# Reordering the start of a fused delta-rule attention and two-layer MLP kernel, with the first MLP product cut into two halves of tokens

## The chip, the cores and the metric

The kernel runs on one core of a Trainium2 chip. The metric is the device time of one execution in microseconds (us). Engines are named as the profile names them: PE is TensorE (PEld its weight loads), DVE is VectorE, ACT is ScalarE, POOL is GpSimd, SP is SyncE, whose queue (SPq) issues nearly all the DMAs. A changed kernel counts here as different from the one before when the times differ by more than 0.3%.

## The reference

Inputs are q, k, v of shape (4, 8, 768, 48) and beta of shape (4, 8, 768), and the weights of two MLPs. For each batch and head a 48x48 state runs over the 768 tokens, and its output feeds the MLPs:

```
k_n = k / (norm(k) + 1e-6)
for t in range(S):
    y[t]  = q[t] @ state
    v_old = k_n[t] @ state
    state = state + beta[t] * outer(k_n[t], v[t] - v_old)
x = y as (3072, 384)
g = elu(x @ w_in);              x1  = g @ w_out        # 384 -> 2048 -> 384
h = x1 @ w2_in
g = h * sigmoid(1.702 * h);     out = g @ w2_out
```

## The kernel before, in words

**Attention.** The tokens of a sequence are cut into 12 chunks of 64 (`c`), and two chunks make a pass (`p`, 6 of them: 4 batches x 128 tokens = 512 columns). Inside a chunk the recurrence is solved in closed form: `gram` gives k.k products (PE, copied out by ACT in one whole copy and two part copies, `far`), `inverse` inverts the triangular matrices of a pass row by row with small DVE instructions (lists of steps: `start`, `take`, `diag`, `root`, `better`, `norm`, `scale`, the rows `step` or `step16`, `finish`, `turn`), `join16` (`left`, `right`), `m1` and `m2` put the blocks together on PE. Then per chunk: `kq` and `mask` (scores), `nv` (v scaled by the norm), `ks` (k times the state, subtracted from v on DVE at L567), `w` (copied out into the tiles su), `state` (the next state, added on DVE at L609), and `ya`, `yb` (the output; `y_out` splits it into xh on ACT and xl on DVE, L655 and L656).

**MLP.** A unit is one pass and one of 16 slices of 128 hidden columns. `up` makes 9 matmuls of 512 columns into a PSUM tile h (two buffers), `elu1` (two ACT instructions) and `elu2` (DVE, L761) follow, `high` (ACT cast to gh, L770) and `low` (DVE, gl, L773) split the result in two numbers, and two units later (`LAG = 2`) `down` makes 9 matmuls into acc0 to acc2. 192 units in all: 96 of layer 0, 96 of layer 1.

**Weights.** `prep` splits each weight slice likewise, once per slice: `rebase` (ACT), `shift` and `rest` (DVE, L714 and L717), `high` (ACT cast to wt, L724) and `low` (POOL, L728 in layer 0). In the list `conv` three entries belong to a slice: shift, rest with high, and low.

**What sets the order.** Everything is issued in an order written by hand; each engine works its own list in order. The code ahead of the units (L931 to L1005) is written out call by call; `also(n)` takes the next n steps of the second inverse. From then on each unit t has lists of things to issue: `fill` (after elu1), `mid` (before elu2), `end` (after down), `tail` (after high). A slot number s in the tables stands for the unit s//2, in `mid` if s is even and in `end` if it is odd. `spread` deals the steps of an inverse out over a stretch of units by the room that `taken` or `slack` leaves.

**PSUM tiles that are waited for.** `wide()` is one tile ps_w of two banks with a single buffer: `gram`, `kq`, `ks`, `w`, `state`, `m2` and y share it, so each waits until the one before has been copied out. While `early` holds, y of chunks 0 and 1 uses the two h buffers instead.

Of the kernel before, what the change touches and what calls it, by code (L numbers as in the profile page):

```python
# [19 lines left out]
P = 128  # L20
NP = S // P
# [10 lines left out]
class Kernel:  # L32
# [433 lines left out]
    def chunk(self, c):  # L466
# [218 lines left out]
    def prep(self, layer, ms, pools):  # L685
# [46 lines left out]
        for j, m in enumerate(ms):  # L732
            t = [lambda m=m: shift(m), lambda m=m: (rest(m), high(m))]
# [3 lines left out]
        steps.append(lambda: low(ms[-1]))  # L737
        return [lambda gate=False, m=m: load(m, gate) for m in ms], [lambda m=m: rebase(m) for m in ms], steps

    def up(self, wt, x, act_fn):  # L740

        nc = self.nc
        xh, xl = x
        hps = self.ps_m.tile([P, TB], F32, name="h", tag="h")
        i = 0
        for k in range(NK):
            for part, src in ((0, xh), (0, xl), (1, xh)):
                nc.tensor.matmul(  # L748
                    hps, wt[:, part, k * P:(k + 1) * P], src[:, k], start=(i == 0), stop=(i == 3 * NK - 1)
                )  # L750
                i += 1
# [105 lines left out]
    def schedule(self):  # L857
# [23 lines left out]
        def spread(where, u0, u1, fns, sizes=None):  # L881
# [3 lines left out]
            if u0 in slack:  # L885
                left = [max(0.2, slack.get(u, 0.0) + (2.8 if u > NM - 3 else 1.2)) for u in range(u0, u1)]
# [31 lines left out]
        loads, bases, conv = self.prep(0, range(NM), lambda m: (self.wp, "wt"))  # L918
        join = {c: self.later(lambda c=c: self.join16(c, home), 6) for c in range(6)}
# [66 lines left out]
        run(conv[0], conv[1], c0["ks"], c0["w"], c1["nv"], conv[2], bases[2], c0["state"])  # L986
# [3 lines left out]
        run(c0["ya"], c1["ks"], conv[3])  # L990
# [34 lines left out]
        for slot in (0, 2, 29, 32):  # L1025
# [3 lines left out]
        at(end, 7, lambda: self.load_v(3))  # L1029
# [5 lines left out]
        for p in range(2, NP):  # L1035
# [3 lines left out]
                (8, a, "kq"), (9, a, "t2"), (10, a, "m1"), (11, a, "ks"), (12, a, "m2"), (14, a, "w"),  # L1039
# [3 lines left out]
            late = 2 if p in self.FINE else 0  # L1043
# [78 lines left out]
    def passes(self, at, spread, half, fill, p, grams, steps, spare=None):  # L1122
# [116 lines left out]
```

## Time and profile before

| | |
|---|---|
| median of 3 runs | 991.79 us (989.93 to 992.45) |
| profiled execution, its own time | 990.37 us |
| its span, first to last instruction | 988.6 us (1.77 us of its time lie outside) |
| mean granted TensorE clock | 0.984 of full speed |
| busy: PE, DVE, ACT, POOL | 941.7, 594.4, 464.2, 83.1 us |
| instructions | 25639 |

Busy times are sums over the whole span. The MLP fills PE from about 92 us on, the attention of later passes runs between its units until about 500 us, and what lies ahead of 92 us is a chain through several engines. So a stretch has to be looked at by itself. The granted clock is 1.00 at 2.4 GHz and 0.50 at 1.2 GHz.

### The profile page before, as it was taken

How to read it: one execution, taken by the hardware profiler on the slowest of the kernel's cores; microseconds unless marked ns; L12 is line 12 of the kernel's file. 1: busy time of each engine (PE TensorE's matmuls, PEld its weight loads, DVE VectorE, ACT ScalarE, POOL GpSimd, SP SyncE). 2: the span in 40 equal slices, each digit the busy share in tenths (PEclk: the TensorE clock that was granted, in tenths of full speed). 3: DMA queues.
4: the chain of work that ended last, by engine and by line, in shares of the span. 5: the costliest groups of instructions: out<-in, count | busy, mean ns of one | idle time of the engine just before them, and what ended most of it. 6: DMA issues, size and time to landing. Idle time of an engine off the chain costs nothing.

```text
span 988.6 us, 25639 instructions
## 1 busy us (share of the span) xinstructions
PE 941.7 (95%) x11520; PEld 773.2 (78%) x11520; DVE 594.4 (60%) x1048; ACT 464.2 (47%) x753; POOL 83.1 (8%) x72
## 2 busy tenths in 40 slices
PE   4866899999999999999999999999999999999998
PEld 4755677778878887888887888888888888888886
DVE  6886887677987877886445676733333333333332
ACT  6636475644374465444446675533333233333332
POOL 3021252010010001000000100101001001010000
PEclk9977999999999999999999999999999999999999
DMA  7263342303211230210114801010010010100000
GB/s 240 88 208 104 108 154 91 114 4 92 83 56 58 74 98 19 92 44 34 34 49 157 371 1 64 1 54 11 1 65 1 1 64 1 64 1 1 33 1 32
DMA packets 20174, 68.33 MB, mean 69 GB/s; under 512 B 3168, under 2 KB 4704, under 8 KB 20064
## 3 DMA queue, kind: packets, MB, share of 16 engines
q1 hardware_dynamic: 19920, 66.56, 20.0%
q8 instruction: 90, 1.47, 0.6%
q14 instruction: 20, 0.16, 0.1%
q10 hardware_dynamic: 144, 0.13, 0.0%
HBM read 57.25 MB, written 9.44 MB: 67 GB/s over the span
## 4 chain that ended last, share of the span: by engine, by line
PE 85%; DVE 8%; ACT 4%; issue 2%; DMA 0%; POOL 0%; ACTq 0%; DVEq 0%; POOLq 0%
PE h L748 38%; PE acc L785 27%; PE accn L785 10%; PE ps_w L562 1%; PE ps_w L504 1%; PE ps_w L579 1%; PE ps_w L602 1%; PE ps_w L629 1%; PE ps_w L203 1%; DVE tmp L317 1%; PE ps_w L645 1%; ACT z L193 1%; DVE t L761 1%; DVE W L322 1%; DVE x L515 1%
## 5 line engine op out<-in xcount | busy, mean ns | idle before, releaser
L748 PE MATMUL h<-xh,wt 128*128 128x512 f32 x1152 | 396.4, 398 | 0.0
L785 PE MATMUL acc<-gh,wt 128*128 128x512 f32 x864 | 292.6, 393 | 0.5 <-DVE xo L846 0.5
L748 PEld LDWEIGHTS h<-xh,wt 128*128 128x128 f32 x1152 | 218.5, 190 | 48.1 <-DVE xl L656 0.2
L748 PE MATMUL h<-xl,wt 128*128 128x512 f32 x576 | 226.6, 393 | 0.0
L773 DVE TENSOR_TENSOR gl<-t,gh 128x512 fp32r<-128x512 f32 x192 | 138.7, 722 | 93.8 <-ACT gh L770 93.6
L785 PEld LDWEIGHTS acc<-gh,wt 128*128 128x128 f32 x864 | 162.7, 188 | 35.7 <-issue 0.9
L770 ACT CAST gh<-t 128x512 fp32r<-128x512 f32 x192 | 119.3, 621 | 118.8 <-DVE t L761 62.2
L785 PE MATMUL acc<-gl,wt 128*128 128x512 f32 x432 | 168.7, 390 | 0.0
L767 DVE TENSOR_TENSOR t<-t,h 128x512 f32<-128x512 f32 x96 | 66.0, 687 | 168.9 <-ACT t L764 168.9
L764 ACT ACTIVATE t<-h 128x512 f32<-128x512 f32 x96 | 57.3, 597 | 187.2 <-PE h L748 187.2
L748 PEld LDWEIGHTS h<-xl,wt 128*128 128x128 f32 x576 | 109.5, 190 | 21.1
L757 ACT ACTIVATE t<-h 128x512 f32<-128x512 f32 x96 | 57.4, 598 | 100.3 <-PE h L748 99.8
L785 PE MATMUL accn<-gh,wt 128*128 128x512 f32 x288 | 96.4, 389 | 0.0
L761 DVE SCALAR_TENSOR_TENSOR t<-t,h 128x512 f32<-128x512 f32 x96 | 65.6, 684 | 51.0 <-ACT t L758 50.5
L785 PEld LDWEIGHTS acc<-gl,wt 128*128 128x128 f32 x432 | 81.4, 188 | 16.1
L785 PEld LDWEIGHTS accn<-gh,wt 128*128 128x128 f32 x288 | 54.1, 188 | 11.3
L758 ACT ACTIVATE t<-t 128x512 f32<-128x512 f32 x96 | 60.7, 632 | 3.1
L812 POOL TENSOR_TENSOR xl<-x1r,xh 128x512 fp32r<-128x512 f32 x18 | 24.1, 1339 | 407.4 <-ACT xh L811 314.4
L785 PE MATMUL accn<-gl,wt 128*128 128x512 f32 x144 | 56.0, 389 | 0.0
L728 POOL TENSOR_TENSOR wt<-w,wt 128x768 fp32r<-128x768 f32 x16 | 31.5, 1974 | 70.7 <-ACT wt L724 70.7
L515 DVE TENSOR_TENSOR x<-ps_w,mask_p 64x512 f32<-64x512 f32 x44 | 30.2, 687 | 11.2 <-PE ps_w L504 10.7
L717 DVE SCALAR_TENSOR_TENSOR w<-raw,w 128x768 uint32<-128x768 uint32 x32 | 35.2, 1101 | 0.9
(190 smaller groups left out, 832.6 us busy)
## 6 DMA issues: line engine op xcount, KB each, us to landing
raw<-in_w SPq DMA_DIRECT2D x32, 768.0 KB, 7.6
kt<-in_kT SPq DMA_DIRECT2D x12, 512.0 KB, 4.5
x<-in_qT SPq DMA_DIRECT2D x24, 256.0 KB, 4.2
kg<-in_kT SPq DMA_DIRECT2D x9, 512.0 KB, 4.8
kn<-in_kn SPq DMA_DIRECT2D x12, 384.0 KB, 3.5
x1d<-xo SPq DMA_DIRECT2D x12, 384.0 KB, 2.9
x1r<-x1d SPq DMA_DIRECT2D x6, 768.0 KB, 4.7
vn<-in_vn SPq DMA_DIRECT2D x11, 384.0 KB, 3.4
```

What stands on the lines that cost most here:

```text
L515: v.tensor_tensor(out=g["x"][k][self.tok(k), 8 * hf:8 * hf + 8], in0=i, in1=self.mask_p[t].unsqueeze(1).to_broadcast(list(i.shape)), op=AL ...
L717: v.scalar_tensor_tensor(out=bits[m], in0=words(m, 0), scalar=29, in1=bits[m], op0=ALU.logical_shift_right, op1=ALU.bitwise_or)
L728: (v if layer else nc.gpsimd).tensor_tensor(out=wt[:, 1], in0=bits.pop(m).bitcast(F32), in1=wt[:, 0].bitcast(F32), op=ALU.subtract)
L748: nc.tensor.matmul(hps, wt[:, part, k * P:(k + 1) * P], src[:, k], start=(i == 0), stop=(i == 3 * NK - 1))
L757: nc.scalar.activation(out=t, in_=hps, func=AF.Relu, scale=-1.0)
L758: nc.scalar.activation(out=t, in_=t, func=AF.Exp, scale=-1.0)
L761: nc.vector.scalar_tensor_tensor(out=t, in0=t, scalar=-1.0, in1=hps, op0=ALU.add, op1=ALU.max)
L764: nc.scalar.activation(out=t, in_=hps, func=AF.Sigmoid, scale=1.702)
L767: nc.vector.tensor_tensor(out=t, in0=t, in1=hps, op=ALU.mult)
L770: nc.scalar.copy(gh, t)
L773: nc.vector.tensor_tensor(out=gl, in0=t, in1=gh.bitcast(F32), op=ALU.subtract)
L785: self.nc.tensor.matmul(self.acc[c], wt[:, part, DM + c * P:DM + (c + 1) * P], src, start=(m == 0 and i == 0), stop=(m == NM - 1 and i == 2),)
```

## The change

The change touches only the order of work, the places of a few PSUM tiles, and one product that is cut in two:

- **Start.** nv of chunk 1 goes ahead of the first weight conversion; the ACT cast `high` of a slice is taken out of `conv` into a list `highs` and stands later; `low` of slice 0 (POOL) goes ahead of y of chunk 0; norm and scale of the second inverse go ahead of `w` of chunk 1, and six row steps (12 DVE instructions) follow it instead of norm, scale and four.
- **Unit 0 in halves.** The new method `first` makes the 9 matmuls of `up` for a range of tokens. The first 256 tokens (chunk 0) are multiplied ahead of `ya` of chunk 1, the other 256 inside unit 0. y of chunk 1 goes to the tiles acc2 and ps_b, since h is now held by the halves.
- **Units 0 to 2.** `state` of chunk 1 goes from the middle of unit 2 to the middle of unit 0, and into acc0 and acc1 instead of ps_w. The two `gram` of pass 2 go from units 0 and 1 to units 1 and 2, each with both of its `far` copies at once. Weight `high` goes into `tail`, behind gh.
- **Later tables.** Items of chunks 2 and 3 move by up to three slots (nv 8 to 7, nv of chunk 3 18 to 21, ks 21 to 22, w 23 to 24, state 25 to 26, y 27 to 28); the `gram` of pass 3 go one slot later; m2 goes ahead of ks in passes 2, 4 and 5 (in pass 3 it already was); pass 5 goes one slot later up to w of its second chunk; `spread` carries a shortage of room over to the next unit.

The core of the diff:

```
-            if first:
+            if c < 2:
                 ps = self.banks(0)
...
-            if self.early:
+            if first:
                 st["y"] = [self.bank(True) for _ in range(2)]
+            elif self.early:
+                st["y"] = [self.ps_m.tile([P, TB], F32, name="acc2", tag="acc2", bufs=1), self.bank()]
...
-            t = [lambda m=m: shift(m), lambda m=m: (rest(m), high(m))]
+            t = [lambda m=m: shift(m), (lambda m=m: (rest(m), high(m))) if layer else (lambda m=m: rest(m))]
...
+    def first(self, wt, x, r, hps=None):
+        xh, xl = x
+        if hps is None:
+            hps = self.ps_m.tile([P, TB], F32, name="h", tag="h")
+        i = 0
+        for k in range(NK):
+            for part, src in ((0, xh), (0, xl), (1, xh)):
+                self.nc.tensor.matmul(
+                    hps[:, r], wt[:, part, k * P:(k + 1) * P], src[:, k, r], start=(i == 0), stop=(i == 3 * NK - 1)
+                )
...
-        run(conv[0], conv[1], c0["ks"], c0["w"], c1["nv"], conv[2], bases[2], c0["state"])
+        run(c1["nv"], conv[0], c0["ks"], c0["w"], conv[1], bases[2], highs[0], c0["state"], conv[4])
...
-        run(c0["ya"], c1["ks"], conv[3])
+        run(conv[2], c0["ya"], c1["ks"], conv[3], highs[1])
         also(1)
         run(c0["yb"])
         also(2)
-        run(bases[3], c1["w"])
+        run(bases[3])
+        also(2)
+        run(c1["w"])
         nc.scalar.activation(out=self.one, in_=self.one, func=AF.Exp)
-        run(conv[4])
         also(6)
+        self.half = self.first(self.wt[0, 0], self.x["a", 0], slice(0, TB // 2))
         run(c1["ya"], c1["yb"])
...
-            at(tail, m - 2, *bases[m + 2:m + 3], *[lambda f=f: f(True) for f in loads[m + 4:m + 5]])
+            at(tail, m - 2, highs[m], *bases[m + 2:m + 3], *[lambda f=f: f(True) for f in loads[m + 4:m + 5]])
...
-                (6, a, "t2"), (6, a, "kq"), (7, a, "m1"), (9 - (p in (3,)), a, "m2"), (8 + (p in (3,)), a, "ks"), (11, a, "w"),
+                (6, a, "t2"), (6, a, "kq"), (7, a, "m1"), (8, a, "m2"), (9, a, "ks"), (11, a, "w"),
...
-            at(half[2], slot // 2, lambda: self.rest[0]())
-            at(fill, slot // 2 + 1, lambda: self.rest[1]())
+            at(half[slot % 2 if p == 2 else 2], slot // 2, lambda: self.rest[0]())
+            at(half[slot % 2] if p == 2 else fill, slot // 2 + (p > 2), lambda: self.rest[1]())
```

Three places show what the engines' lists look like. A row is one instruction: line, operation, output and inputs, shape and count. The first place is PE behind `w` of chunk 1 (its last row is the first below; x_196, x_197 are q of chunk 1, su_90, su_94 its state). Before, y of chunk 1 follows at once:

```order
L579 MATMUL acc_974<-raw,z 64x48 x2
L629 MATMUL h<-x_196,su_90 32x64 x4
L629 MATMUL h<-x_197,su_94 32x64 x8
L629 MATMUL h<-x_196,su_90 32x64 x8
L629 MATMUL h<-x_197,su_94 32x64 x8
L629 MATMUL h<-x_196,su_90 32x64 x4
```

After the change the nine matmuls of the first half stand there, ahead of y, which goes to another tile:

```order
L751 MATMUL h<-xh,wt 128x256
L751 MATMUL h<-xl,wt 128x256
L751 MATMUL h<-xh,wt 128x256 x2
L751 MATMUL h<-xl,wt 128x256
L751 MATMUL h<-xh,wt 128x256 x2
L751 MATMUL h<-xl,wt 128x256
L751 MATMUL h<-xh,wt 128x256
L631 MATMUL acc_1044<-x_196,su_90 32x64 x4
```

The other half (nine such rows) stands behind y, where the nine matmuls of 512 columns stood, and the 32 matmuls of `state` of chunk 1 stand right behind it.

The second place is ACT from elu1 of unit 0 on (t<-h, t<-t) to the next weight cast. Before, the weight cast (L724) and the whole copy of the first gram (L190) stand ahead of gh (L770), and its part copies (L193) come one at a time, each behind elu1 or gh of a unit:

```order
L757 ACTIVATE t<-h 128x512
L758 ACTIVATE t<-t 128x512
L724 CAST wt<-w 128x768
L190 COPY z<-ps_w 128x1024
L770 CAST gh<-t 128x512
L707 ACTIVATE raw<-raw 128x768
L702 COPY raw<-one 128x1
L193 COPY z<-ps_w 32x1024
L757 ACTIVATE t<-h 128x512
L758 ACTIVATE t<-t 128x512
L724 CAST wt<-w 128x768
L193 COPY z<-ps_w 32x1024
```

After, from the same elu1 of unit 0, the weight cast (L726) stands behind gh (L783), and the three copies of the gram stand together behind elu1 of unit 1:

```order
L770 ACTIVATE t<-h 128x512
L771 ACTIVATE t<-t 128x512
L783 CAST gh<-t 128x512
L726 CAST wt<-w 128x768
L709 ACTIVATE raw<-raw 128x768
L704 COPY raw<-one 128x1
L770 ACTIVATE t<-h 128x512
L771 ACTIVATE t<-t 128x512
L190 COPY z<-ps_w 128x1024
L193 COPY z<-ps_w 32x1024 x2
```

The third place is DVE in units 9 to 11, from the output of chunk 2 on (xl<-ps_w). Before, the subtraction of `ks` of chunk 3 (vn<-vn,ps_w) follows after one elu2:

```order
L656 TENSOR_TENSOR xl<-ps_w,xh 128x3x256
L761 SCALAR_TENSOR_TENSOR t<-t,h 128x512
L567 TENSOR_TENSOR vn<-vn,ps_w 128x768
L714 TENSOR_SCALAR w<-raw 128x768
L717 SCALAR_TENSOR_TENSOR w<-raw,w 128x768
L773 TENSOR_TENSOR gl<-t,gh 128x512
```

After, nv of chunk 3 has come to this place and ks has moved behind the weight conversion and gl; on PE its matmuls stand behind up of unit 11 instead of ahead of it:

```order
L658 TENSOR_TENSOR xl<-ps_w,xh 128x3x256
L774 SCALAR_TENSOR_TENSOR t<-t,h 128x512
L490 TENSOR_TENSOR vn<-vn,ntok 128x768
L716 TENSOR_SCALAR w<-raw 128x768
L719 SCALAR_TENSOR_TENSOR w<-raw,w 128x768
L786 TENSOR_TENSOR gl<-t,gh 128x512
L567 TENSOR_TENSOR vn<-vn,ps_w 128x768
```

## Rows read from the trace of the kernel before

**Rows 1.** The page, busy time, share of the span and instructions of each engine.
```profile
PE 941.7 (95%) x11520; PEld 773.2 (78%) x11520; DVE 594.4 (60%) x1048; ACT 464.2 (47%) x753; POOL 83.1 (8%) x72
```

**Rows 2.** Stretches: length, busy by engine, granted clock, DMA share, GB/s.
```profile
54.30:67.96 13.66, 9.70 (x179) 7.56 (x178) 12.19 (x31) 3.53 (x7) 3.50 (x2) 0.50 0.67 190
...
88.50:91.90 3.40, 3.40 (x69) 2.91 (x62) 2.04 (x4) 0.00 (x0) 0.59 (x1) 0.51 0.30 92
...
149.90:153.30 3.40, 3.40 (x16) 2.65 (x9) 2.98 (x4) 0.98 (x2) 0.00 (x0) 0.50 1.04 325
153.30:988.00 834.70, 827.72 (x8454) 677.44 (x8452) 476.40 (x820) 374.90 (x591) 41.70 (x32) 1.00 0.16 53
```

**Rows 3.** Timeline of PE: start, duration, instruction, idle before and its releaser.
```profile
58.94 1.72 PE L629 MATMUL h<-x,su 128*32 128x64 f32 x56 [1.72 <-DVE su L586]
...
62.46 1.44 PE L645 MATMUL h<-x,su 128*32 128x64 f32 x42 [1.17 <-issue]
...
79.12 1.99 PE L203 MATMUL ps_w<-kg 48*64 48x64 f32 x64 [7.71 <-ACT z L193]
...
88.29 1.47 PE L602 MATMUL ps_w<-su,kn 64*48 64x48 f32 x64 [3.10 <-ACT z L193]
...
92.93 1.26 PE L395 MATMUL ps_b<-xl,z 32*32 32x16 f32 x128
...
129.54 0.50 PE L748 MATMUL h<-xh,wt 128*128 128x512 f32 x1
...
148.87 1.18 PE L562 MATMUL ps_w<-su,kt 48*64 48x48 f32 x64 [2.24 <-DVE xl L656]
...
383.37 0.22 PE L457 MATMUL ps_w<-m,kg 32*32 32x32 f32 x2 [1.32 <-DVE vn L567]
```

**Rows 4.** Chain that ended last: start, duration, line; nine matmuls of one up.
```profile
81.11 4.10 PE h L748 x9
...
94.19 2.26 PE h L748 x9
```

**Rows 5.** Timeline of DVE and POOL, 54 to 123 us.
```profile
54.23 3.57 POOL L728 TENSOR_TENSOR wt<-w,wt 128x768 fp32r<-128x768 f32 x2
...
56.12 1.73 DVE L282 SCALAR_TENSOR_TENSOR nb<-nb,na 128x32 f32<-128x32 f32 x1
...
60.86 0.21 DVE L301 STREAM_TRANSPOSE ntok<-nb 128x32 f32<-128x32 f32 x1
...
64.68 0.55 DVE L714 TENSOR_SCALAR w<-raw 128x768 uint32<-128x768 uint32 x1
...
65.27 0.96 DVE L717 SCALAR_TENSOR_TENSOR w<-raw,w 128x768 uint32<-128x768 uint32 x1
...
67.35 0.28 DVE L317 TENSOR_TENSOR tmp<-W 128x112 f32<-128x112 f32 x1
...
76.08 1.96 DVE L336 STREAM_TRANSPOSE xl<-W 128x1024 f32<-128x1024 f32 x1
...
77.88 0.67 DVE L773 TENSOR_TENSOR gl<-t,gh 128x512 fp32r<-128x512 f32 x1
...
89.81 2.25 DVE L609 TENSOR_TENSOR su<-su,ps_w 48x384 f32<-48x384 f32 x4 [5.76 <-PE ps_w L602]
...
121.72 0.69 DVE L761 SCALAR_TENSOR_TENSOR t<-t,h 128x512 f32<-128x512 f32 x1
```

**Rows 6.** Timeline, 115 to 117 us: a POOL subtraction and a DVE transpose beside it.
```profile
115.11 1.86 POOL L728 TENSOR_TENSOR wt<-w,wt 128x768 fp32r<-128x768 f32 x1 [7.89 <-ACT wt L724]
...
115.73 1.24 DVE L433 STREAM_TRANSPOSE xh<-z 128x1024 f32<-128x1024 f32 x1
```

**Rows 7.** Timeline of ACT, 75 to 83 us.
```profile
75.03 1.00 ACT L193 COPY z<-ps_w 32x1024 f32<-32x1024 f32 x1
...
77.22 0.81 ACT L724 CAST wt<-w 128x768 fp32r<-128x768 f32 x1
...
82.08 0.62 ACT L770 CAST gh<-t 128x512 fp32r<-128x512 f32 x1
```

More of the change, by code (lines that the diff above doesn't have):

```diff
@@ L737, in prep @@
         steps.append(lambda: low(ms[-1]))
+        self.highs = [lambda m=m: high(m) for m in ms]
         return [lambda gate=False, m=m: load(m, gate) for m in ms], [lambda m=m: rebase(m) for m in ms], steps
-    def up(self, wt, x, act_fn):
-        nc = self.nc
+    def first(self, wt, x, r, hps=None):
         xh, xl = x
-        hps = self.ps_m.tile([P, TB], F32, name="h", tag="h")
+        if hps is None:
+            hps = self.ps_m.tile([P, TB], F32, name="h", tag="h")
         i = 0
@@ L747, in up @@
             for part, src in ((0, xh), (0, xl), (1, xh)):
-                nc.tensor.matmul(
-                    hps, wt[:, part, k * P:(k + 1) * P], src[:, k], start=(i == 0), stop=(i == 3 * NK - 1)
+                self.nc.tensor.matmul(
+                    hps[:, r], wt[:, part, k * P:(k + 1) * P], src[:, k, r], start=(i == 0), stop=(i == 3 * NK - 1)
                 )
                 i += 1
+        return hps
+    def up(self, wt, x, act_fn):
+        nc = self.nc
+        if self.half is None:
+            hps = self.first(wt, x, slice(0, TB))
+        else:
+            hps, self.half = self.half, None
+            self.first(wt, x, slice(TB // 2, TB), hps)
         t = self.mp.tile([P, TB], F32, name="t", tag="t", bufs=3)
@@ L852, in run @@
         self.early = True
+        self.half = None
         self.pools()
@@ L885, in spread @@
             if u0 in slack:
-                left = [max(0.2, slack.get(u, 0.0) + (2.8 if u > NM - 3 else 1.2)) for u in range(u0, u1)]
+                left, over = [], 0.0
+                for u in range(u0, u1):
+                    over += slack.get(u, 0.0) + (2.8 if u > NM - 3 else 1.2)
+                    left.append(max(0.2, over))
+                    over -= left[-1]
             part, u, room = sum(left) / sum(sizes), u0, left[0]
@@ L1009, in schedule @@
             at(fill, m - 2, *conv[3 * m - 1:3 * m + 2])
-            at(tail, m - 2, *bases[m + 2:m + 3], *[lambda f=f: f(True) for f in loads[m + 4:m + 5]])
+            at(tail, m - 2, highs[m], *bases[m + 2:m + 3], *[lambda f=f: f(True) for f in loads[m + 4:m + 5]])
             taken[m - 2] = 0.37
         at(fill, NM - 2, conv[-1])
-        at(end, 2, lambda: self.load_kn(2))
-        for slot, c, i in ((4, 2, 0), (5, 2, 1), (7, 2, 3), (7, 3, 0), (8, 3, 1), (10, 3, 3)):
+        at(end, 1, lambda: self.load_kn(2))
+        for slot, c, i in ((4, 2, 0), (5, 2, 1), (7, 2, 3), (8, 3, 0), (8, 3, 1), (10, 3, 3)):
             at(end if slot % 2 else mid, slot // 2, *[join[c][k] for k in part[i]])
@@ L1024, in schedule @@
             use(slot, name)
-        for slot in (0, 2, 29, 32):
+        for slot in (2, 4, 30, 33):
             use(slot, "gram")
@@ L1028, in schedule @@
             spread(fill, 0, 3, [f for _, f in beside], [size for size, _ in beside])
-        at(end, 7, lambda: self.load_v(3))
+        at(end, 8, lambda: self.load_v(3))
         at(end, 9, lambda: self.load_kn(3))
@@ L1038, in schedule @@
             first = (
-                (8, a, "kq"), (9, a, "t2"), (10, a, "m1"), (11, a, "ks"), (12, a, "m2"), (14, a, "w"),
+                (8, a, "kq"), (9, a, "t2"), (10, a, "m1"), (12, a, "ks"), (11, a, "m2"), (14, a, "w"),
             ) if p in self.FINE else (
-                (6, a, "t2"), (6, a, "kq"), (7, a, "m1"), (9 - (p in (3,)), a, "m2"), (8 + (p in (3,)), a, "ks"), (11, a, "w"),
+                (6, a, "t2"), (6, a, "kq"), (7, a, "m1"), (8, a, "m2"), (9, a, "ks"), (11, a, "w"),
             )
-            late = 2 if p in self.FINE else 0
+            late = 2 if p in self.FINE else int(p == NP - 1)
+            first = tuple((slot + (p == NP - 1), c, name) for slot, c, name in first)
             turn = (17, 15) if p in (3,5,) else (15, 17)
@@ L1063, in schedule @@
             if p == 2:
-                self.passes(at, spread, (mid, end, tail), fill, p, (0, 2), (6, o + 2), lambda: turned(2))
+                self.passes(at, spread, (mid, end, tail), fill, p, (2, 4), (6, o + 2), lambda: turned(2))
             else:
-                grams = (29, 32) if p == 3 else (2 * o - 32, 2 * o - 29)
+                grams = (30, 33) if p == 3 else (2 * o - 32, 2 * o - 29)
                 self.passes(at, spread, (mid, end, tail), fill, p, grams, (o - 11 if p == 3 else o - 13, o + 3))
```

1 line of the change is left out of this document (added), and 6 rows, old and new, of the table v1.

## The prediction, made before the changed kernel ran

> **What bounds the kernel now.** The first view is the page's table of busy times: PE works 941.7 of 988.6 us [rows 1], so the end moves only with what PE waits for or does slowly. The second is the table of stretches, cut where the granted clock changes. From 153.3 us on PE is busy 827.72 of 834.70 us at clock 1.00 [rows 2]: there is little left there. Ahead of that lie three stretches at half clock, 13.66, 3.40 and 3.40 us long [rows 2]. The third view, PE's timeline with its waits, says why. Between 58 and 93 us PE idles 1.72 us for the copies of `w` of chunk 1 on DVE (L586), 1.17 us for nothing shown ("issue"), 7.71 us and 3.10 us for the part copies of the two gram on ACT (L193) [rows 3]: 13.7 us. What runs right after such a gap runs slowly: nine matmuls of an up take 4.10 us in unit 2 and 2.26 us in unit 3 [rows 4]. Later two single waits stand out, 2.24 us ahead of `ks` of chunk 3 at 148.87 us and 1.32 us ahead of `m2` of pass 4 at 383.37 us [rows 3]. So the change is worth what it takes out of these places, provided that DVE, which is nearly as busy there, doesn't become the new wait.
>
> **The change part by part.** Both gram waits come from part copies that ACT reaches only behind elu1, gh and weight casts of the next units. After the change ps_w is free when unit 0 begins (state and y of chunk 1 no longer use it), and the three copies of a gram, about 1.00 us each [rows 7], stand together. That takes PE out of the wait. The next thing that PE must wait for is then `left` of chunk 2, which needs the transposed inverse (`turn`, L336). It ended at 78.04 us (76.08 + 1.96) [rows 5], while PE took `left` only at 92.93 us [rows 3]. So I follow DVE to the end of `turn`.
>
> *Step 1, copies of w.* Two POOL subtractions side by side, 3.57 us, held two DVE instructions up; one of them took 1.73 us where one of that shape takes 0.21 [rows 5]. One of the two subtractions now runs earlier: 1.52 us less. But norm and scale now stand ahead of the copies: from 58.94 us [rows 3] to 61.07 us (60.86 + 0.21) [rows 5], 2.13 us. y of chunk 1 therefore starts at 58.94 - 1.52 + 2.13 = 59.55 us, 0.6 us later than before. The first half of unit 0 fills PE's gap ahead of it and costs nothing while that gap is longer than it: 1.72 us before, some 2.3 us now, against 2.05 us (half of 4.10 [rows 4], as 256 columns are half of 512).
>
> *Step 2, PE behind the copies.* y of chunk 1 took from 58.94 to 63.90 us (62.46 + 1.44) [rows 3], 4.96 us with the issue gap; I keep the gap: 64.5 us. The second half, 2.05 us: 66.6 us. `state`, 1.47 us [rows 3]: 68.0 us. No trace shows a matmul of 256 columns; from below a half costs 1.13 us (half of 2.26), from above a whole 4.10 us [rows 4], if the loads and not the columns set the pace. I take 2.05 since the stretch to 67.96 us is at clock 0.50 [rows 2]. The Trainium skill (TensorE: Matmul & The Clock Gate, Back-to-back issue gap) gives columns divided by 1.2 GHz at the lower level, 213 ns for 256, an estimate of 1.92 us for nine, and the sum would be 0.13 us better; but its section LDWEIGHTS says that a load goes by the 128 columns of the weights, whatever the moving width, which speaks against halves: nine loads more, by its 107 ns an estimate of 0.96 us where they aren't hidden. No run here shows that yet.
>
> *Step 3, DVE's wait for state.* The addition of `state` (L609) now stands in unit 0. DVE reached the end of `rest` of slice 2 at 66.23 us (65.27 + 0.96) [rows 5], 7.29 us behind the copies. After the change that is less by norm and scale (2.13) and more by three pairs of row steps (3 x 2 x 0.28 [rows 5] = 1.68), from 59.5 us on: 66.35 us. DVE then waits 1.65 us for state at 68.0.
>
> *Step 4, turn.* Against 78.04 us: 1.52 less (step 1), 1.65 more (step 3), and the work that moved ahead of it: the addition 2.25, gl of unit 0 0.67, elu2 of unit 1 0.69, shift and rest of slice 4 0.55 + 0.96 [rows 5], together 5.12. Norm and scale only change places. It ends at 83.3 us, and `left` starts there instead of at 92.93: 9.6 us earlier. A POOL subtraction (`low` of slice 3) can fall beside `turn`. If it held a transpose up as it holds additions, that would cost 1.86; but a transpose beside one took 1.24 us and ended with it [rows 6], so it ran on, and I take 0.
>
> *Step 5, the rest of PE's list before left.* elu2 of unit 0 ends near 68.0 + 2.25 + 0.69 = 70.9 us; behind it ACT does gh 0.62, the weight cast 0.81, three instructions that I bound by 1.00 each and three copies of 1.00 [rows 7]: 78.4 us at the latest. The second gram takes at most 1.99 us [rows 3], down of unit 0 2.26 to 4.10 us [rows 4]: 82.7 to 84.5 us. That is inside 83.3 or up to 1.2 us late; I take 0.
>
> *Step 6, clock.* PE will again have idled ahead of `left`, and what follows may run at half clock as between 88.5 and 91.9 us: 3.40 us at 0.51, of which 1.7 are lost [rows 2]. I charge it whole. The start gives 9.6 - 1.7 = 7.9 us. From above, without the issue gap and the clock loss, 10.8; from below, with 1.7, 1.86, 1.2 and a half that costs a whole (2.05 more) taken off 9.6, 2.8.
>
> *Step 7, ks of chunk 3.* Ahead of it stood one `down`, 2.26 us, and then 2.24 us of wait. Now an up stands there too, another 2.26 us [rows 4], which just covers it. With the wait the half-clock stretch at 149.9 us should go, 3.40 us at 0.50, another 1.7 [rows 2]. I take 3.9; from below 0, if the copies of y are late by as much again.
>
> *Step 8, m2 of pass 4.* It waited for the subtraction of `ks` (L567) because ks stood just ahead of it. The order is turned round: m2 follows m1 after an up, ks follows m2 after a down, 2.26 us of cover each. I take 1.3, from below 0.
>
> *Step 9, costs.* Nine more matmuls and loads, and slots that moved by one or two: 0.5 us, from 0 to 3 (the length of the largest waits that remain of this kind [rows 3]).
>
> Sum: 7.9 + 3.9 + 1.3 - 0.5 = 12.6 us off the profiled execution's own 990.37 us: 977.8 us. The median of the runs lies 1.4 us above that execution, so a median after would lie between 977.8 and 979.2; I say 978.5.
>
> **The rivals.** *Only one of the two places gains.* Either DVE, which has only shifted its work, holds the units after `left` (start 2.8, steps 7 and 8 whole), or the start gains and the later waits come back at their new slots (7.9 and nothing). For it: the cover of step 7 is exact to 0.02 us. Against it: before, DVE itself waited 5.76 us for PE at 89.81 us [rows 5], so it had room. 990.37 - 8.0 + 0.5 or 990.37 - 7.9 + 0.5, both near 983 us. *The change doesn't do what it says:* transposes are held up, halves cost as much as wholes, and the later waits return: 990.37 - 2.8 + 0.5 = 988 us, no change that can be told. Rows 6 speaks against it. *Slower:* the weight cast `high` now waits in `tail` behind gh and so behind elu2 on DVE. From the end of elu2 to wt complete it takes 0.62 + 0.81 [rows 7] + 1.86 [rows 6] = 3.3 us, and up two units later needs it; before, the cast waited for neither. It decides once elu2 ends less than 3.3 us before that up is due. Before, the time between was 7.1 us for unit 6 (121.72 + 0.69 [rows 5] to 129.54 [rows 3]). If DVE fell back so far that PE lost 1.2 us in each of the 14 units that cast weights, that is 17 us: 990.37 - 12.6 + 17 = 995 us. Against it: elu2 moves ahead of seven pairs of row steps in unit 0.
>
> **How the numbers follow.** I give the forecast 0.63, the first rival 0.25, no change 0.07, slower 0.05. About 0.3% (3 us) is what a measurement of this kernel can tell from no change, so faster has 0.63 + 0.25 = 0.88. The forecast's own bounds are 990.37 - 16.0 = 974.4 (10.8 + 3.9 + 1.3) and about 983; the range must take in most of the first rival and the 1.4 us between execution and median: 973.5 to 986.5.
>
> **What would show it.** Step 1: DVE's copies of w end near 59.5 us, PE fills the gap ahead of them with nine matmuls. Step 2: those take about 2 us, not 4. Steps 3 to 5: no wait of PE for L193; `turn` ends near 83 us with `left` behind it. Step 7: no wait ahead of ks of chunk 3 and no half clock near 140 us. Step 8: none ahead of m2 of pass 4. The prediction is wrong if PE waits for POOL's `low` ahead of an up, or if `left` comes later than 88 us.

## The result: 980.0 us, and the profile after

| | before | after |
|---|---|---|
| median on the same chip, us | 990.93 (4 executions, 989.93 to 992.45) | 980.0 (4 executions: 978.1, 978.35, 981.66, 981.95) |
| ratio | | 0.9889, interval 0.9859 to 0.9918 |
| profiled execution: own time, span, us | 990.37, 988.6 | 981.95, 980.2 |

The change is faster by 1.1%, 1.5 us behind the forecast of 978.5 us and inside its range. The profiled execution of after is the slowest of its four; a second profile, taken in a later run of the same kernel (e8 below), has a span of 977.9 us.

The busy times of after answer to [rows 1]: PE's work is the same but for the nine extra matmuls, and the span is 8.4 us shorter.

```profile
PE 942.6 (96%) x11529; PEld 773.2 (79%) x11529; DVE 600.7 (61%) x1048; ACT 463.7 (47%) x753; POOL 83.3 (9%) x72
```

The table of stretches, to be read against [rows 2] (length, busy by engine, granted clock, DMA share, GB/s):

```profile
54.60:58.00 3.40, 3.37 (x51) 3.09 (x50) 3.08 (x11) 2.12 (x3) 0.00 (x0) 0.54 1.06 347
61.40:68.20 6.80, 5.73 (x125) 5.24 (x125) 3.11 (x7) 1.60 (x3) 0.00 (x0) 0.52 0.36 102
75.00:85.30 10.30, 7.03 (x77) 5.36 (x77) 9.89 (x22) 7.80 (x12) 1.85 (x1) 0.52 0.61 222
130.00:160.00 30.00, 29.40 (x541) 22.87 (x540) 29.17 (x49) 18.84 (x30) 12.01 (x6) 1.00 0.41 135
184.30:191.10 6.80, 6.80 (x122) 5.60 (x110) 2.69 (x6) 1.84 (x3) 0.00 (x0) 0.52 0.01 2
191.10:980.00 788.90, 783.82 (x7664) 641.88 (x7662) 445.49 (x756) 346.27 (x548) 35.53 (x29) 1.00 0.15 52
```

The half clock at 149.9 us is gone, as forecast: 130 to 160 us run at 1.00. But a new stretch at half clock stands at 184.3 us, 6.8 us long.

PE's timeline (start, duration, instruction, idle before and its releaser) shows the start:

```profile
55.82 0.58 PE L751 MATMUL h<-xh,wt 128*128 128x256 f32 x1
...
58.04 1.18 PE L631 MATMUL acc<-x,su 128*32 128x64 f32 x64
59.04 0.39 PE L647 MATMUL ps_b<-x,su 128*32 128x64 f32 x13
62.47 1.71 PE L647 MATMUL ps_b<-x,su 128*32 128x64 f32 x51 [3.04 <-issue]
64.11 0.58 PE L751 MATMUL h<-xh,wt 128*128 128x256 f32 x1
...
66.33 1.53 PE L602 MATMUL acc<-su,kn 64*48 64x48 f32 x64
...
72.30 0.50 PE L751 MATMUL h<-xh,wt 128*128 128x512 f32 x1 [0.75 <-ACT wt L726]
...
74.25 0.73 PE L751 MATMUL h<-xh,wt 128*128 128x512 f32 x2 [1.22 <-POOL wt L730]
...
79.98 1.99 PE L203 MATMUL ps_w<-kg 48*64 48x64 f32 x64 [3.27 <-DMA kg<-in_kT]
81.90 0.79 PE L798 MATMUL acc<-gh,wt 128*128 128x512 f32 x1
...
85.85 1.26 PE L395 MATMUL ps_b<-xl,z 32*32 32x16 f32 x128
```

Read it against [rows 3]. The wait for the copies of `w` and both waits for the gram copies (L193) are gone, and `left` (L395) starts 7.1 us earlier. In their place stand three: for the late weight cast of slice 2 (0.75 and 1.22 us), and 3.27 us for a load, key half 1 for the second gram. The idle time for nothing shown inside y of chunk 1 has grown, from 1.17 to 3.04 us. Why the load is late, SP's queue shows:

```profile
73.16 0.33 SPq L705 DMA_DIRECT2D raw<-in_w  x1
...
74.06 0.38 SPq L151 DMA_DIRECT2D kg<-in_kT  x1
```

It is issued behind the load of weight slice 6, which the program gates behind a small copy on ACT (L704, 72.95 us).

VectorE's part, against [rows 5], and a POOL subtraction beside `turn`:

```profile
56.80 1.08 DVE L586 COPY su<-acc 64x384 f32<-64x384 f32 x2
...
67.90 2.25 DVE L609 TENSOR_TENSOR su<-su,acc 48x384 f32<-48x384 f32 x4 [0.89 <-PE acc L602]
...
80.95 2.05 DVE L336 STREAM_TRANSPOSE xl<-W 128x1024 f32<-128x1024 f32 x1
81.03 1.85 POOL L730 TENSOR_TENSOR wt<-w,wt 128x768 fp32r<-128x768 f32 x1 [6.83 <-DVE w L719]
```

Later, three waits of PE stand where before had none:

```profile
170.70 1.16 PE L203 MATMUL ps_w<-kg 48*64 48x64 f32 x64 [0.85 <-ACT z L193]
174.60 0.50 PE L798 MATMUL acc<-gl,wt 128*128 128x512 f32 x1 [0.24 <-DVE gl L786]
183.97 1.58 PE L410 MATMUL ps_b<-w 16*32 16x16 f32 x128 [1.76 <-DVE w L384]
```

The timeline of all engines ahead of the last of them:

```profile
178.13 1.01 ACT L193 COPY z<-ps_w 32x1024 f32<-32x1024 f32 x1
...
178.74 1.02 DVE L859 COPY xo<-acc 128x512 f32<-128x512 f32 x2
179.16 1.00 ACT L857 COPY xo<-acc 128x512 f32<-128x512 f32 x2
179.78 0.34 SPq L839 DMA_DIRECT2D x1d<-xo  x1
...
180.56 1.02 SPq L840 DMA_DIRECT2D x1d<-xo  x1
...
183.11 0.71 DVE L384 STREAM_TRANSPOSE w<-kg 128x512 f32<-128x512 f32 x1 [1.70 <-DMA x1d<-xo]
```

The join of chunk 6 (L384, then L410) writes into a buffer that the writes of x1 to memory must have left. The copies that feed those writes (L857) stand on ACT behind a part copy of the second gram of pass 3 (L193). They stood so in before too, but without a wait:

```profile
180.01 1.16 PE L203 MATMUL ps_w<-kg 48*64 48x64 f32 x64
...
188.48 1.00 ACT L844 COPY xo<-acc 128x512 f32<-128x512 f32 x2
...
192.95 0.81 PE L410 MATMUL ps_b<-w 16*32 16x16 f32 x74
```

From the start of the gram to the end of these copies it takes 9.5 us in both kernels (180.01 to 189.48, 170.70 to 180.16). On PE it took 12.94 us from the gram to the join in before, and in after 13.27 with 1.76 and 0.24 us of waits, so 11.27 without them. The gram, a slot later, now stands behind a `down` that it had stood ahead of. So PE has 1.7 us less to do between gram and join, while the way to the end of the copies is as long as it was.

### The profile page after: what moved, and what is told of

It is laid out like the page before. It is cut to its first block, busy times and chain, and to the rows that moved or that the text cites. A ratio compares the mean times of both kernels' runs of the same rounds, so it can differ in the third digit from the quotient of the medians.

```text
span 980.2 us, 25674 instructions
## 1 busy us (share of the span) xinstructions
PE 942.6 (96%) x11529; PEld 773.2 (79%) x11529; DVE 600.7 (61%) x1048; ACT 463.7 (47%) x753; POOL 83.3 (9%) x72
## 3 DMA queue, kind: packets, MB, share of 16 engines
q8 instruction: 90, 1.47, 0.6%
## 4 chain that ended last, share of the span: by engine, by line
PE 83%; DVE 11%; ACT 3%; issue 2%; DMA 1%; SPq 0%; DVEq 0%; ACTq 0%
PE h L751 37%; PE acc L798 26%; PE accn L798 10%; PE ps_w L504 1%; DVE t L774 1%; DVE gl L786 1%; PE ps_w L562 1%; PE ps_w L579 1%; DVE W L322 1%; DVE w L719 1%; PE ps_w L631 1%; PE ps_w L203 1%; DVE tmp L317 1%; PE ps_w L647 1%; ACT z L193 1%
## 5 line engine op out<-in xcount | busy, mean ns | idle before, releaser
L751 PE MATMUL h<-xh,wt 128*128 128x512 f32 (+1 forms) x1158 | 396.4, 397 | 2.6 <-POOL wt L730 1.7
L751 PE MATMUL h<-xl,wt 128*128 128x512 f32 (+1 forms) x579 | 226.8, 392 | 0.0
L786 DVE TENSOR_TENSOR gl<-t,gh 128x512 fp32r<-128x512 f32 x192 | 141.7, 738 | 88.7 <-ACT gh L783 88.5
L783 ACT CAST gh<-t 128x512 fp32r<-128x512 f32 x192 | 119.3, 621 | 142.4 <-DVE t L774 86.0
L770 ACT ACTIVATE t<-h 128x512 f32<-128x512 f32 x96 | 57.3, 597 | 93.1 <-PE h L751 92.7
```

Of the source, the lines that this page charges most:

```text
L751: self.nc.tensor.matmul(hps[:, r], wt[:, part, k * P:(k + 1) * P], src[:, k, r], start=(i == 0), stop=(i == 3 * NK - 1))
L770: nc.scalar.activation(out=t, in_=hps, func=AF.Relu, scale=-1.0)
L783: nc.scalar.copy(gh, t)
L786: nc.vector.tensor_tensor(out=gl, in0=t, in1=gh.bitcast(F32), op=ALU.subtract)
```

## The experiments

The first four kernels shared runs of before with a median of 992.11 us, the next four 991.58 us, the last four 994.15 us.

**e1: no half ahead of y.**

```diff
-        self.half = self.first(self.wt[0, 0], self.x["a", 0], slice(0, TB // 2))
```

> The changed kernel, but unit 0's first product in one piece of 512 columns behind y of chunk 1 (the half ahead of y is left out; nothing else moves). Theory A (the halves lie on the path: behind y come the product, state, DVE's addition, elu2, the gated weight load and the load of k for the second gram): PE needs 2.2 us more behind y, left of chunk 2 starts 2.2 us later, the time goes up by about 2 us, to 982. Theory B (the half only fills a gap that DVE sets, and the end of turn or the load decide anyway): no change, 980 within 0.5 us.

983.04 us (6 executions, 979.58 to 987.07), ratio 0.9906 (0.9882 to 0.9929). PE waits for the copies of `w` again, and the time is 2 to 3 us over after (by the ratios and by the medians), with intervals that overlap. Yet unit 2 starts at 72.95 us against 72.30, and `left` at 85.60 us against 85.85. The second profile of after (e8) has `left` at 84.36, so these profiles alone can't tell whether the half saves up to 1.2 us there; e11 below can. What e1 loses against after, it loses later: 1.64 us at 101.66 us, where the profile shows nothing waited for, and 2.55 us (after: 1.76) at the join of chunk 6.

**e2: the load of weight slice 6 a unit later.**

```diff
-            at(tail, m - 2, highs[m], *bases[m + 2:m + 3], *[lambda f=f: f(True) for f in loads[m + 4:m + 5]])
+            at(tail, m - 2, highs[m], *bases[m + 2:m + 3])
+            at(tail, max(1, m - 2), *[lambda f=f: f(True) for f in loads[m + 4:m + 5]])
```

> The changed kernel, but the gated load of weight slice 6 moves from the tail of unit 0 to the tail of unit 1, so that the load of k for the second gram of pass 2 is issued ahead of it. Theory A (PE's 3.27 us ahead of the second gram are the load alone, and turn is done 2.8 us before left): the load starts near 71.7 us in place of 74.1, the wait shrinks to under 1 us, left starts near 83.2 us, the time falls by 2 to 2.7 us. Theory B (half clock or the inverse hold that stretch whatever the load does): under 0.5 us.

979.95 us (978.2 to 981.89), ratio 0.9877 (0.9858 to 0.9896). The wait for the load is gone, and `left` waits for `turn`, as step 4 had it:

```profile
77.92 1.97 PE L203 MATMUL ps_w<-kg 48*64 48x64 f32 x64
...
83.42 1.26 PE L395 MATMUL ps_b<-xl,z 32*32 32x16 f32 x128 [1.26 <-DVE xl L336]
...
181.48 1.53 PE L410 MATMUL ps_b<-w 16*32 16x16 f32 x128 [1.63 <-DVE w L384]
```

`left` is 2.4 us earlier than in after, the span 2.2 us shorter; the median hardly shows it. The wait for the join stays.

**e3: the part copies of the gram of pass 3 at once.**

```diff
-            at(half[slot % 2 if p == 2 else 2], slot // 2, lambda: self.rest[0]())
-            at(half[slot % 2] if p == 2 else fill, slot // 2 + (p > 2), lambda: self.rest[1]())
+            at(half[slot % 2 if p <= 3 else 2], slot // 2, lambda: self.rest[0]())
+            at(half[slot % 2] if p <= 3 else fill, slot // 2 + (p > 3), lambda: self.rest[1]())
```

> The changed kernel, but the two part copies of each gram of pass 3 are issued at once with the whole copy, as for pass 2. Theory A (moving these grams one slot later put their part copies ahead of the copies of x1 on ACT, so x1's write, the release of its buffer, the transposes of chunk 4 and right come late: 0.85 and 1.76 us of waiting and in some executions a half-clock stretch of 6.8 us that loses 3.4): the waits ahead of the second gram and of right shrink to under 0.5 us each, no half clock near 185 us, all executions near 976 to 977.5. Theory B (the write of x1 itself takes that long, or the half clock comes and goes without the wait): 979 to 980, still two groups of times.

978.22 us (977.73 to 979.16), ratio 0.986 (0.9843 to 0.9877). The wait for the join falls to 0.53 us and the half clock behind it is gone.

**e4: the slots of chunks 2 and 3 and of the gram of pass 3 as before.**

```diff
...
-            (13, 2, "m1"), (12, 2, "ks"), (15, 2, "m2"), (16, 2, "w"), (18, 2, "state"), (21, 3, "nv"),
-            (20, 2, "ya"), (20, 2, "yb"), (22, 3, "ks"), (24, 3, "w"), (26, 3, "state"), (28, 3, "ya"), (28, 3, "yb"),
+            (13, 2, "m1"), (12, 2, "ks"), (15, 2, "m2"), (16, 2, "w"), (18, 2, "state"), (18, 3, "nv"),
+            (20, 2, "ya"), (20, 2, "yb"), (21, 3, "ks"), (23, 3, "w"), (25, 3, "state"), (27, 3, "ya"), (27, 3, "yb"),
...
-                grams = (30, 33) if p == 3 else (2 * o - 32, 2 * o - 29)
+                grams = (29, 32) if p == 3 else (2 * o - 32, 2 * o - 29)
```

> The changed kernel, but the items of chunks 2 and 3 from unit 3 on and the grams of pass 3 stand in the slots of before; the start, the halves, m2 ahead of ks and pass 5 stay changed. Theory A (steps 7 and 8 of the prediction): the 2.24 us wait ahead of ks of chunk 3 and its half-clock stretch return (3.9 us), the wait of 1.76 us ahead of right and its half clock go (1.8 to 5 us): 979 to 982. Theory B (the later tables gain nothing, the start gives all): 976 to 978, with no wait ahead of ks.

980.87 us (980.3 to 981.37), ratio 0.9885 (0.9869 to 0.9902): the old slots make the time of the changed kernel. The wait ahead of `ks` of chunk 3 is back, 138 to 144 us run at 0.50, and in exchange the join waits 0.43 us and has no half clock behind it.

```profile
138.12 1.96 PE L562 MATMUL ps_w<-su,kt 48*64 48x48 f32 x64 [2.34 <-DVE xl L658]
...
184.57 1.56 PE L410 MATMUL ps_b<-w 16*32 16x16 f32 x128 [0.43 <-DVE w L384]
```

**e5: the order of m2 and ks as before in passes 2, 4 and 5** (the shift of pass 5's slots, which its expectation names too, stayed as in after).

```diff
-                (8, a, "kq"), (9, a, "t2"), (10, a, "m1"), (12, a, "ks"), (11, a, "m2"), (14, a, "w"),
+                (8, a, "kq"), (9, a, "t2"), (10, a, "m1"), (11, a, "ks"), (12, a, "m2"), (14, a, "w"),
...
-                (6, a, "t2"), (6, a, "kq"), (7, a, "m1"), (8, a, "m2"), (9, a, "ks"), (11, a, "w"),
+                (6, a, "t2"), (6, a, "kq"), (7, a, "m1"), (9 - (p in (3,)), a, "m2"), (8 + (p in (3,)), a, "ks"), (11, a, "w"),
```

The first pair is pass 2, the second passes 3 to 5 (pass 3 keeps its order).

> The changed kernel with the order of `m2` and `ks` in passes 2 and 4, and the slots of pass 5, as before the change. Theory A (the order of `m2` and `ks` is a gain of its own): PE waits about 1.3 us for the product of values of chunk 8 again, as in the row of before at 383 us, and the time is 1.0 to 2.0 us over that of the changed kernel on the same chip. Theory B (the start gives all of the gain, later waits are swallowed by slack): the wait may be there, the time is within 0.5 us of the changed kernel.

985.17 us (980.59 to 987.3), ratio 0.9925 (0.9903 to 0.9947), 6.2 us over after on the same chip (e8): more than either theory. The wait is 1.84 us, and this time half clock follows it:

```profile
378.00:380.00 2.00, 2.00 (x102) 0.61 0.03 8
380.00:382.00 2.00, 2.00 (x7) 0.53 0.00 0
```

From unit 52 to unit 54 PE takes 15.67 us (369.99 to 385.66), against 12.22 in after: 3.45 us more. Against the profile of e8, which is 6.7 us shorter, e5 is 2.7 us late at unit 20 already, ahead of the places that the edit moves; another 0.9 us goes by unit 24, where PE idles 1.02 us for nothing shown ahead of L457 at 211.37 us, and e8 doesn't. What the 6.2 us between the medians are made of, one profile can't tell.

**e6: e2 and e3 together.**

> The changed kernel with the two waits that it brought taken away together: the load of weight block 6 a unit later, so that the load of key half 1 for the second gram is not behind it, and the copies of the gram rows of pass 3 run at once, so that those of chunk 6 are not ahead of the states' copies of pass 3. Theory A (the give-backs are separate and add up: about 2 us at the second gram and 3.5 us near 184 us, as the two edits alone showed 1.7 to 2.2 us off the span and 2.8 us): no wait of PE over 1.2 us for kg or for the join of chunk 6, and 975 to 977 us. Theory B (they overlap: with one of them gone the other wait grows, since both edits only move PE earlier against the same copies and writes): 977.5 to 978.5 us, no better than the better of the two alone.

976.32 us (975.49, 975.7, 976.94, 980.13), ratio 0.9854 (0.9836 to 0.9873). Both waits are gone, as A had it, and it is 2.6 us under after on the same chip (e8). The profiled execution is the slowest of the four; it has idle times of 0.44 and 1.83 us for nothing shown, near 95 and 100 us, and half clock behind the second (0.50 from 102 to 104 us).

**e7: the start of before, with the later tables, the order of m2, pass 5 and the `spread` of after.**

```diff
-        run(c1["nv"], conv[0], c0["ks"], c0["w"], conv[1], bases[2], highs[0], c0["state"], conv[4])
+        run(conv[0], conv[1], c0["ks"], c0["w"], c1["nv"], conv[2], bases[2], c0["state"])
...
-            (0, 1, "state"), (6, 2, "kq"), (6, 2, "mask"), (7, 2, "nv"), (9, 3, "kq"), (9, 3, "mask"), (11, 2, "t2"),
+            (4, 1, "state"), (6, 2, "kq"), (6, 2, "mask"), (7, 2, "nv"), (9, 3, "kq"), (9, 3, "mask"), (11, 2, "t2"),
...
```

> The start of before (no half product ahead, casts and copies in the old order, the state of chunk 1 at unit 2) with the later tables, the order of `m2` and `ks` and pass 5 of after. Theory A (the new start and the later tables are separate gains): of the 10 to 11 us the start's 7 to 8 are gone, the 3.9 at the values of chunk 3 and the 1.3 of pass 4 stay, less what the copies near 184 us give back (0 to 5): 985 to 991 us. Theory B (the later tables gain only with the new start, since without it the gram rows and joins fall a slot late against the old start): 991 us or more, no half clock lost near 140 us but new waits of PE at the joins of pass 3.

991.71 us (12 executions, 988.43 to 993.9), ratio 1.0 (0.9987 to 1.0012): nothing gained, as theory B had it. There is no wait at `ks` of chunk 3, and unit 12 starts at 151.38 us against 156.87 in before, 5.5 us earlier. By unit 20 it is 0.6 us, and the wait is at a join of pass 3, as B said. Its reason doesn't hold: B put the wait down to the old start, but after, with the new one, waits there too.

```profile
192.00 1.25 PE L410 MATMUL ps_b<-w 16*32 16x16 f32 x128 [2.34 <-DVE w L384]
```

and behind that wait the clock is halved (stretches of 2 us, busy PE, granted clock):

```profile
194.00:196.00 2.00, 2.00 (x6) 0.50 0.00 0
```

**e8: the changed kernel once more.**

> The changed kernel unaltered, on the same chip as the three others, for comparison with them. Theory A (its two groups of times of 978.2 and 981.8 us come from the wait for the join of chunk 6 near 184 us, with the half clock behind it there in one group and not in the other): both groups are seen again, and a profile with the half clock at 184 to 191 us stands near 980 us or above. Theory B (chance of the chip alone): the profile has that half clock whatever its time.

978.94 us (978.02 to 980.17), ratio 0.9874 (0.986 to 0.9888). The profiled execution (979.58 us) waits 1.54 us at the join, and the half clock behind it is shorter:

```profile
182.00:184.00 2.00, 1.74 (x129) 0.78 0.03 8
184.00:186.00 2.00, 2.00 (x6) 0.50 0.00 0
186.00:188.00 2.00, 2.00 (x9) 0.87 0.00 0
188.00:190.00 2.00, 2.00 (x92) 1.00 0.00 0
```

This doesn't tell the theories apart: both profiles of this kernel are of the slower half of their runs, and both have the half clock, with a length that differs. The start differs by 1.5 us too (unit 3 at 85.55 us against 87.04), so not all of the scatter comes from the join.

**e9: e7 with the copies of e3.**

> The kernel before with only the later tables, the order of `m2` and `ks` and pass 5 of the change (991.71 us, no faster than before, in the run ahead of this one), and now the copies of the gram rows of pass 3 at once as well. Theory A (the 5.5 us that the later tables gained by unit 12 were given back at the copies of the gram rows of pass 3, which stand ahead of the states' copies and hold the join of chunk 6): PE waits 1 us or less for the join, no half clock at 192 to 200 us, and 985 to 988 us. Theory B (the join is held by something that does not move with these copies, such as the transfer of the states itself or the work of VectorE up to there): the wait stays and the time is 990 us or more.

988.65 us (9 executions, 985.79 to 989.95), ratio 0.9941 (0.992 to 0.9962), where e7 had 1.0. PE no longer waits for the join, and the clock there stays at 1.00:

```profile
192.00:198.00 6.00, 6.00 (x150) 1.00 0.01 3
```

The same stretch of e7 is at 0.72. Theory A. The time is half a microsecond above its 985 to 988, on a chip where before itself was 2.6 us slower.

**e10: e6 with the order of m2 of e5.**

> The version with both waits taken away (976.3 us in the run ahead of this one), with the order of `m2` and `ks` in passes 2, 4 and 5 as before the change. Theory A (the wait alone is lost, as it was in before, 1.3 us with the clock kept): 1.0 to 2.0 us over that version. Theory B (PE comes to `m2` of pass 4 with a different distance to VectorE and the half clock follows the wait, as in the run that undid the order alone, 2.8 plus 1.3 us there): 3.0 to 5.0 us over it.

982.45 us (979.51 to 987.54), ratio 0.989 (0.9857 to 0.9923). A wait of 1.79 us, and 372 to 376 us at 0.57; unit 52 to 54 takes 15.78 us against 12.21 in e6. Theory B by the trace (3.6 us); the median lies 6.1 us over e6, which ran on another occasion, and 7.3 over e12 on the same chip. In the profile 1.4 us more go between units 20 and 24 (27.45 us, 26.07 in e12), with 1.28 us of idle time for nothing shown ahead of L457 at 204.71 us.

**e11: e6 without the half ahead of y.**

> The version with both waits taken away, without the half product ahead of y of chunk 1 (the first product whole, behind `y` and the copies). Theory A (the half is worth 3 us by itself, as its removal from the changed kernel cost 3.1): 2.5 to 3.5 us over that version. Theory B (behind the half the load of key half 1 was the next wait in the changed kernel, and hid part of it; with that wait gone the half is worth its full 2 us of product plus the wait of 2.2 for the copies of `w`, 4 us or more): 4 to 5 us over it. Theory C (the turn holds `left` in this version, so what the half saves ahead of it is swallowed): 1 us or less over it.

980.26 us (978.46 to 985.38), ratio 0.9875 (0.9843 to 0.9906), 3.9 us over e6 and 5.1 over e12 on the same chip. But `left` starts at 82.58 us, against 82.96 in e12, 83.03 in e10 and 84.05 in e6, which have the half: up to there theory C holds, while the median lies between theories A and B. The loss comes behind it, where the profile shows idle time for nothing and then half clock:

```profile
94.28 1.09 PE L395 MATMUL ps_b<-xl,z 32*32 32x16 f32 x108 [1.08 <-issue]
```

```profile
96.00:98.00 2.00, 2.00 (x7) 0.50 0.31 125
```

**e12: e6 with the weight cast of slice 2 early.**

```diff
-            at(tail, m - 2, highs[m], *bases[m + 2:m + 3])
+            at(fill if m == 2 else tail, m - 2, highs[m])
+            at(tail, m - 2, *bases[m + 2:m + 3])
```

> The version with both waits taken away, and the high part of weight block 2 cast at the start of unit 0 on ScalarE, not at its end, so that the product of unit 2 does not wait for it (1.08 and 1.21 us in that version's profile). Theory A (these waits are hidden behind the turn that `left` of chunk 2 needs, which VectorE sets): within 0.7 us of that version. Theory B (with the load for the second gram out of the way they are on the path): 1 to 2.3 us faster.

975.15 us (6 executions, 974.82 to 977.52), ratio 0.9817 (0.9793 to 0.9841), the best of all kernels here. The waits for the cast are gone, but PE waits 3.04 us for a gram copy instead, and `left` comes no earlier than in e10:

```profile
77.83 1.86 PE L203 MATMUL ps_w<-kg 48*64 48x64 f32 x64 [3.04 <-ACT z L193]
82.96 1.26 PE L395 MATMUL ps_b<-xl,z 32*32 32x16 f32 x128 [0.17 <-DVE xl L336]
```

By the trace that is theory A; its median is 1.2 us under that of e6, which ran on another occasion (by the ratios, 0.9817 against 0.9854, it is 3.7 us), so this doesn't tell the two apart.

Where each kernel's units start (first matmul of the unit's up, us) shows what was kept:

| unit | before | after | e8 | e3 | e4 | e7 | e9 | e10 | e12 |
|---|---|---|---|---|---|---|---|---|---|
| 3 | 94.12 | 87.04 | 85.55 | 88.68 | 85.59 | 94.12 | 93.97 | 84.22 | 84.15 |
| 20 | 200.84 | 193.72 | 190.46 | 190.41 | 191.56 | 200.27 | 196.79 | 185.96 | 185.88 |
| 52 | 376.37 | 369.28 | 366.28 | 366.36 | 367.97 | 376.14 | 373.93 | 363.32 | 361.85 |
| 54 | 389.96 | 381.50 | 378.63 | 378.77 | 380.66 | 388.91 | 386.14 | 379.10 | 374.07 |
| 191 | 976.43 | 968.00 | 965.66 | 965.22 | 967.38 | 975.57 | 972.90 | 965.57 | 960.90 |

## Why the prediction was right, and which step of it failed

The time and the sign were right, and the start is where the gain is: e7 without it gains nothing, e4 with it and the old slots gains as much as after. The sum was not right in its parts: it promised 12.6 us off the profiled execution, and the two profiled executions differ by 8.4 (990.37 to 981.95). No run undoes the earlier `state`, the moved grams of pass 2 and their joined copies one by one; that these free the start rests on the two waits for L193 that are gone from the traces.

*Steps 1 to 4, the chain to turn.* The copies of `w` ended at 57.88 us (56.80 + 1.08), not 59.5: the way to them on DVE became 3.1 us shorter ahead of norm and scale (L288 at 54.94 us, 59.13 in before behind 1.11 us of copies), not 1.52. Behind them the idle time inside y, kept at 1.17 us, was 3.04. These two errors largely cancel, and that the second half could start near the forecast 64.5 us (at 64.11) is luck. A half took 2.22 us (55.82 to 58.04, and 64.11 to 66.33) against 2.05; `state` ended at 67.86 us against 68.0; DVE waited 0.89 us instead of 1.65; `turn` ended at 83.0 us against 83.3, and the POOL subtraction beside it didn't hold it up (2.05 us, against 1.96 in [rows 5]). The matmuls of a half start 0.21 us apart, but for 0.38 us behind the first. The Trainium skill (TensorE: Matmul & The Clock Gate, Back-to-back issue gap) gives columns divided by 1.2 GHz at the lower level, an estimate of 213 ns for 256, and the trace agrees. The loads, which the Trainium skill (TensorE: Matmul & The Clock Gate, LDWEIGHTS) counts by 128 columns, show no extra time between these matmuls.

*Step 2's half product is not what pays.* e11 shows that taking it away doesn't delay `left`, which DVE sets there, and e1, where the load sets it, shows nothing against that. Nor does y of chunk 1 end later without it: behind its idle time for nothing shown it goes on at 62.46 us in before [rows 3], 62.47 in after and 62.15 in e1. That idle time does not keep its length. It ends 7.57 to 8.12 us behind the end of the idle time ahead of it in 11 of the 14 profiles (8.66 to 9.76 in e3, e5 and e9), with the half or without: 7.57 us in before and e11, 7.84 in after and e12. So what the half filled ahead of y was lost in y. What is lost without it, 2 to 5 us in the medians, is lost later. In the profiles of e1 and e11 idle times for nothing shown have a part in it (1.64 and 1.08 us, the second with half clock behind it), and the last section says what they are. Since e6, with the half, has such times too, it stays open how much of the difference the half makes.

*Step 5 failed.* It took 0 for the rest of PE's list: `left` came 2.55 us behind 83.3. The step counted copies and matmuls and left out the load of key half 1, whose place in SP's queue is behind a gated weight load. e2 shows it: with the load free, `left` starts at 83.42 us behind `turn`. Step 6's charge of 1.7 us for the clock behind `left` fell away (86 us on is at 1.00), so the start gave 7.1 us (unit 3) where 7.9 was forecast.

*Step 7 was right in its place and wrong in what it is worth.* The wait and its half clock are gone, but e7 and e4 show that the 3.9 us didn't stay: the later slots on the old start give a ratio of 1.0, and the old slots on the new start the same time as the new ones. Between unit 3 and unit 20 after gained nothing on before. The loss is in **step 9**, "costs 0.5 (0 to 3)", the term that was mis-sized: 0.85 + 0.24 + 1.76 us of waits and 6.8 us at half clock, of which some 3.3 are lost (clock 0.52), 6.1 us in all. Against it stand step 7's gain and idle times for nothing shown, which took 4.2 us of before between these units (1.60, 1.48 and 1.00 us the largest) and 1.0 us of after; the prediction had no term for these 3.2 us, and without them after would have lost here. That the copies of the pass 3 gram cause the wait, e3 shows on after (0.53 us left) and e9 on e7 (none left). In time only e9 shows it: 0.9941 against 1.0, with intervals apart, while the interval of e3 overlaps that of after. This is the rival "the start gains and the later waits come back at their new slots", at another line.

*Step 8* held: 1.4 us between units 52 and 54 (7.1 ahead of before, then 8.5). Undoing it costs more, 3.5 us in e5 and 3.6 in e10, since the wait there now brings half clock with it, which in before it did not.

*The rival of the late weight cast* appeared in small: PE did wait for POOL's `low` ahead of the up of unit 2 (1.22 us), which the prediction named as a sign of being wrong. e12 shows that it cost nothing up to `left`.

That the forecast of 978.5 came near 980.0 is in part luck. For the profiled execution the sum had 977.8 us and the rival of the returning waits about 983; it took 981.95, nearer to the rival, and the second profile (e8) 979.58. The execution of before that the sum started from is near its median, while the one of after is 1.95 us above its own.

## What to carry to other kernels

A slot moved later to cover one wait carries its copies along: list what stands behind them on their engine, and which buffer waits for that, before booking the gain. When PE's wait is replaced, follow every operand of the next instruction to its issue, and past which gated entries of the queue its load stands. And undo each part on the final kernel: the half product looked like the heart of this change and did not bring `left` forward, and the two best kernels (e6 and e12) came from clearing the two waits that the change had made. An idle time for which the profile names nothing is no constant either: add work ahead of it and see whether it ends later or only gets shorter.

## What the runs showed of the hardware that was not expected

PE stops in the middle of a group of alike matmuls, waiting for nothing that the profile shows, at places that go by a count. In before the two gaps near 55 and 62 us stand 42 (rest of L579) + 64 (L629) + 22 (L645) = 128 matmuls apart; in after, with nine matmuls of the half between, 42 + 9 + 64 + 13 = 128 again: the second gap has moved from 42 matmuls ahead of the end of its group to 51. All 14 profiles have these two gaps behind the same numbers of matmuls, 1238 and 1366.

The second gap of before is in [rows 3], that of after in PE's timeline above; these are the first of before and, behind it, the first of after:

```profile
54.89 1.41 PE L579 MATMUL acc<-raw,z 64*64 64x48 f32 x42 [2.66 <-issue]
```

```profile
54.63 1.26 PE L579 MATMUL acc<-raw,z 64*64 64x48 f32 x42 [3.96 <-issue]
```

Likewise e6 stops with 117 matmuls of a `left` to go and e11, nine matmuls shorter, with 108. Among the DMA queues of after one carries instructions, 1.47 MB in 90 packets, 16.3 KB each; the second line is the same queue from 52.3 to 53.4 us, inside the first gap:

```profile
q8 instruction: 90, 1.47, 0.6%
```

```profile
q8 instruction: 1, 0.02, 5.5%
```

The trace's times of these packets say what PE stood for. In after one takes from 52.34 to 53.30 us, and PE goes on at 54.63; the next from 59.95 to 61.23, and PE goes on at 62.47. The 14 profiles have 66 idle times of PE above 0.35 us for nothing shown, and every one ends 1.23 to 1.60 us behind the end of such a packet, of which there is one in about 11 us. So these idle times are waits for the next block of instructions: the gaps of y, those of before between units 3 and 20, those of e1, e6 and e11, and those ahead of L457 in e5 and e10.

The Trainium skill (Runtime: NRT & Kernel Launch, Instruction fetch mechanics) says that instructions come in blocks of 16 KiB, 256 instructions, and that crossing a boundary is mostly hidden. The size agrees: 128 matmuls with a weight load each are 256 instructions. The cost doesn't: the first of these gaps took 2.35 to 4.51 us in the profiles here, the second 0.99 to 3.85. Why a block comes late is not shown. During the first gap the DMA engines are full (a share of 0.98 to 1.00 from 50.7 to 54.6 us in after), but during the gap of 1.83 us that ends at 100.61 us in e6 they were idle (0.00), with its packet from 98.23 to 99.19 us. How much of the scatter between executions comes from this stays open; of the 3.8 us by which the profile of e6 lies above its median, 1.83 us are that gap.
